# Earlier loads, copies moved to the scalar engine and re-spaced weight pieces in a DFT and mixture-of-experts kernel

## The chip, the cores and the metric

The kernel runs on one core of one Trainium2 chip, as one program. The metric is the device time of that core in microseconds (us). Its engines run beside each other, each through its own list of instructions in order, and meet at semaphores: TensorE (PE for matrix products, PEld for the loads of its stationary operand), VectorE (DVE), ScalarE (ACT), GpSimd (POOL), and SyncE (SP), which here issues nearly all DMA transfers. An instruction that waits holds up everything behind it on its engine, and a transfer that waits holds up every later transfer of SP.

## The reference

The batch is 8 sequences of 3072 tokens with 256 features, in float32.

1. A real DFT along each sequence. The spectrum is mixed by a complex 256x256 matrix (`w_r`, `w_i`) and a bias, every real and imaginary part is shrunk towards zero by 0.01, and an inverse DFT gives `y`.
2. `h = y @ w_in` (256 to 2048), `g = h - tanh(h)`, `x = g @ w_out` (2048 to 256). `w_in` and `w_out` come as float64.
3. A soft mixture of experts: logits `x @ phi` (32 slots), a softmax over all tokens to form slot inputs, eight small experts on them, and a softmax over slots to give each token its output.

## The kernel before, in words

**Phases.** `kernel_body` (L1435) runs a spectral phase (step 1), a token phase (step 2 and the logits and sums of step 3) and an expert phase. The change is all in `spectral_phase` (L125 to L631). The two are generators: the spectral one yields once per step, and beside its last steps `kernel_body` draws the first pieces of the token phase (`TOKENS_BESIDE`, L43).

**The DFT in pieces.** 3072 = 96 x 32. `f1_half` (L234) makes the 96-point part of half a piece of the input `x`; its result goes to DRAM as `ad` (a store through `flush`, L151, at the head of the next step). `load_a2` (L263) brings it back regrouped, 512 KB for two steps, into a pool of three buffers (`fa2`, L138). `f2_pair` (L275) makes the 32-point part for one step (8 small products, L281) into the PSUM bank `f2`, of which there is one. `mix_part` (L324) multiplies by the mixing matrix in three parts of six products, `add_bias` (L342) and `shrink` (L359) finish the spectrum, `i1_pair` (L374) does the first part of the inverse; its result goes to DRAM as `vd`, comes back by `load_v2` (L386) and `i2_half` (L397) does the second part into `yt`, stored as `yd`.

**The order is written by hand.** One loop, L576 to L631, has T = 96 steps (8 sequences of 12) and 12 more to drain. Step s does `f2_pair` for s, mixing, bias and shrinking for s-1, `i1_pair` for s-2, and pieces of `f1` for the next sequence and of `i2` for the one before. Each call puts its instructions at the ends of the engines' lists and its transfers at the end of SP's, so the order of calls in a step is the order on every engine. Within a step: `flush`, `f2_pair`, one chore, new chores (`narrow`), `load_x`, `mix_part` 0, `add_bias`, `load_v2`, half of `f1`, some `i2`, `fold_w`, `use_w`, `load_wf`, `split_sum`, three chores, `mix_part` 1 and 2, the other half of `f1`, `shrink`, two chores, the rest of `i2`, `i1_pair`, `store_y`, `load_a2`, `load_w`.

**The weights' pieces.** 32 pieces (16 of `w_out`, then 16 of `w_in`, L420) are prepared beside the DFT. For a piece due at step t, `load_w` (L428, at t) brings 256 KB of float64 into `raw`, of which there is one buffer; `narrow` (L497, from t+1) turns it into float32 by 11 operations of VectorE, the chores, which `pump` (L492) hands out over the steps; `use_w` (L437, at t+4) transposes it on TensorE into the bank `f2` (L453) and copies it out to `wt` (L455); `fold_w` (L466, at t+5) multiplies `wt` into the bank `f2` again and takes that out (L488 for `w_out`; L478 and L480 for `w_in`). `load_wf` (L458, at t+3) brings what the `w_in` pieces are multiplied with. The bank `f2` is thus shared by `f2_pair`, `use_w` and `fold_w`: each waits until what the one before left there has been read out.

**When things come.** A sequence's pieces of `w` are due at its steps 1, 3, 5 and 7 (L572). `load_a2` is called two steps before its data is used (L623). Before the loop, L526 to L539 make `f1` for the first sequence and load tables (`f2`, `i1`, `bias`) and the first `a2`.

Of the kernel before, what the change touches and what calls it, by code (L numbers as in the profile page):

```python
# [12 lines left out]
AF = mybir.ActivationFunctionType  # L13
ALU = mybir.AluOpType
# [110 lines left out]
def spectral_phase(tc, nb, x, w_r, w_i, b_r, b_i, tb, yd, w_in, w_out, phi, ident, wo32, md, wh, wl, wp, wy, ew):  # L125

    nc = tc.nc
    with ExitStack() as late, ExitStack() as mid, ExitStack() as ctx:
# [53 lines left out]
        def load_f2(g0, g1):  # L182
            nc.sync.dma_start(out=f2[:, 128 * g0:128 * g1], in_=tb["f2"][:, 128 * g0:128 * g1])
# [33 lines left out]
        def load_tables():  # L217
            nc.sync.dma_start(out=i1, in_=tb["i1"])
            nc.sync.dma_start(out=bias[:, 0:256], in_=b_r.partition_broadcast(128))
            nc.sync.dma_start(out=bias[:, 256:512], in_=b_i.partition_broadcast(128))  # L220
            nc.gpsimd.memset(dh.bitcast(F32), 0.0)
            nc.gpsimd.memset(dl_.bitcast(F32), 0.0)
# [214 lines left out]
        def use_w(j):  # L437
            src, r, q = pieces[j]
            t = wnew.pop(j)
            if src is w_in:  # L440
                n = slice(256 * (q % 2), 256 * (q % 2) + 256)
                if wl[r][q // 2] is None:
                    wl[r][q // 2] = ew.wp.tile([128, 512], F32R, tag=f"wl{r}{q // 2}", name="wl")
                h = wh[r][q // 2][:, n]
                nc.scalar.activation(h, t, AF.Copy)
                nc.gpsimd.tensor_tensor(
                    out=wl[r][q // 2][:, n], in0=t, in1=h.bitcast(F32), op=ALU.subtract
                )
            else:
                nc.sync.dma_start(out=wo32[128 * r:128 * r + 128], in_=t)  # L450
            pt = ps.tile([128, 2, 128], F32, tag="f2", name="pt", bufs=1)
            for k in range(2):
                nc.tensor.transpose(pt[:, k, :], t[:, 128 * k:128 * k + 128], ident)  # L453
            wt = dcp.tile([128, 2, 128], F32, tag="wt", name="wt")
            nc.vector.tensor_copy(wt, pt)  # L455
            wtr[j] = wt

        def load_wf(j):  # L458
            src, r, q = pieces[j]
            if src is w_in:  # L460

                home, tag = (ew.wp, "wl13") if j < 26 else (ew.gp, "g4")
                wf = wfs[j] = home.tile([128, 2, 256], F32, tag=tag, name="wf")
                nc.sync.dma_start(out=wf, in_=wo32[256 * q:256 * q + 256].rearrange("(k p) m -> p k m", p=128))

        def fold_w(j):  # L466

            src, r, q = pieces[j]
            wt = wtr.pop(j)
            if src is w_in:  # L470
                pw = ps.tile([128, 288], F32, tag="f2", name="pw", bufs=1)
                wf = wfs.pop(j)
                for k in range(2):
                    F = 2 * q + k
                    nc.tensor.matmul(pw[:, 0:256], wt[:, k, :], wf[:, k], start=k == 0, stop=k == 1, skip_group_check=True)
                    nc.tensor.matmul(pw[:, 256:288], wt[:, k, :], wp[:, F, :], start=False, stop=k == 1, skip_group_check=True)
                if q == 0:
                    nc.vector.tensor_scalar(out=mw, in0=pw, scalar1=-1.0, scalar2=None, op0=ALU.mult)  # L478
                else:
                    nc.vector.tensor_tensor(out=mw, in0=mw, in1=pw, op=ALU.subtract)  # L480
                if q == 7:
                    nc.sync.dma_start(out=md[128 * r:128 * r + 128], in_=mw[:, 0:256])
                    nc.vector.tensor_copy(wy[:, r], mw[:, 256:288])
                return
            pw = ps.tile([128, 32], F32, tag="f2", name="pw", bufs=1)
            for k in range(2):
                nc.tensor.matmul(pw, wt[:, k, :], ph[:, k, :], start=k == 0, stop=k == 1)
            nc.vector.tensor_scalar(out=wp[:, r, :], in0=pw, scalar1=-1.0, scalar2=None, op0=ALU.mult)  # L488

        chores = []  # L490

# [34 lines left out]
        if True:  # L526
            load_f2(0, 2)
            for i in range(8):
                for j in range(2):
                    f1_half(0, i, j)  # L530
                if i == 2:
                    load_mix()
            split_mix()
            load_a2(0, 0)
            load_f2(2, 8)
            load_tables()
            load_f2(8, 16)
            load_f2(16, NG)
            load_late_tables()  # L539
            T = nb * NP  # L540

            pieces_at = {}
            for k in range(1, nb):
                for j in range(8):
                    pieces_at[NP * (k - 1) + j + (2 if k == 1 else 0)] = (k, j)

            def piece(t):
                return [pieces_at[t]] if t in pieces_at else []

            for t in range(3):  # L550
                for j in piece(t):
                    load_x(*j)

            i2_at, v2_at, y_steps = {}, {}, {}
            for k in range(nb):
                t = NP * k + NP
                if k < nb - 2:
                    steps = [t + 4 + j for j in range(4)] + [t + 8 + j // 2 for j in range(8)] + [t + 12 + j for j in range(4)]
                    gap = 1
                else:  # L560
                    steps = [t + 4 + j // 2 for j in range(16)]
                    gap = 1
                for j in range(8):
                    for u in range(2):
                        i2_at.setdefault(steps[2 * j + u], []).append((k, j, u))
                    v2_at.setdefault(max(t + 3, steps[2 * j] - 3), []).append((k, j))
                for h in range(2):
                    for u in range(3):
                        t1 = steps[8 * h + 7] + 1 + gap * u
                        y_steps.setdefault(t1 if k < nb - 1 else T + NP - 1, []).append((k, h, 2 * u))  # L570

            slots = [NP * k + j for k in range(nb) for j in range(1, 9, 2)]  # L572
            due_w = {}
            for j in range(len(pieces)):
                due_w.setdefault(slots[len(slots) * j // len(pieces)], []).append(j)
            for s in range(T + NP):  # L576
                b, i = divmod(s, NP)
                flush()
                if s < T:
                    f2_pair(b, i)  # L580
                pump(1)
                for j in due_w.get(s - 1, ()):
                    narrow(j)
                for j in piece(s + 3):
                    load_x(*j)
                m = divmod(s - 1, NP) if 1 <= s <= T else None
                if m:
                    mix_part(*m, 0)
                    add_bias(*m)
                for j in v2_at.get(s, ()):  # L590
                    load_v2(*j)
                for j in piece(s):
                    f1_half(*j, 0)
                due = i2_at.get(s, ())
                for j in due[:(len(due) + 1) // 2]:
                    i2_half(*j)
                for j in due_w.get(s - 5, ()):
                    fold_w(j)
                for j in due_w.get(s - 4, ()):
                    use_w(j)  # L600
                for j in due_w.get(s - 3, ()):
                    load_wf(j)
                if s < T:
                    split_sum(b, i)
                pump(3)
                if m:
                    mix_part(*m, 1)
                if m:
                    mix_part(*m, 2)
                for j in piece(s):  # L610
                    f1_half(*j, 1)
                if m:
                    shrink(*m)
                pump(2)
                for j in due[(len(due) + 1) // 2:]:
                    i2_half(*j)
                if 2 <= s <= T + 1:
                    i1_pair(*divmod(s - 2, NP))
                for j in y_steps.get(s, ()):
                    store_y(*j)  # L620
                if 4 <= s < 12:
                    load_i2(s - 4)
                if s + 2 < T:  # L623
                    load_a2(*divmod(s + 2, NP))
                for j in due_w.get(s, ()):
                    load_w(j)
                if s == T:
                    ctx.close()
                if s == T + 3:
                    mid.close()  # L630
                yield  # L631
# [865 lines left out]
```

## Time and profile before

| | |
|---|---|
| three runs, us | 2300.38, 2306.78, 2307.19; median 2306.78 |
| the profiled execution's own time | 2304.85 us |
| its span, first to last instruction | 2302.7 us (2.15 us lie around it) |
| granted TensorE clock, mean over the span | 0.989 |
| busy: PE, PEld, DVE, ACT, POOL | 97%, 79%, 76%, 63%, 29% |
| the spectral steps 0 to 95 | from 28.7 to about 692 us |

How to read it: one execution was recorded. "Idle before" an instruction is the time its engine stood still ahead of it, and the arrow names whose event ended that; where several were awaited it is the one that came last. The granted clock is the share of full speed that TensorE was given: 1.0 is 2.4 GHz, 0.5 is 1.2 GHz.

### The profile page before, as it was taken

The page shows a single profiled execution, that of the slowest core. Times are in us where ns is not written, and L with a number is a line of the kernel's source. Part 1 is how long each engine was busy: PE and PEld are TensorE (multiplying, and loading weights), DVE is VectorE, ACT ScalarE, POOL GpSimd, SP SyncE. Part 2 cuts the span into 40 slices and gives each one's busy share as a digit, 9 for nine tenths or more (in the row PEclk, how much of TensorE's full clock was granted, in tenths as well). Part 3 has the DMA queues.
Part 4 walks back from the last instruction along what each step waited for, and adds up shares of the span by engine and source line. Part 5 has one row for each costly group of instructions (what it writes and reads, how often), then busy time and mean ns, then how long its engine had stood idle before and what let it go on. Part 6 is the DMA issues. An engine that isn't in the chain of part 4 may idle for free.

```text
span 2302.7 us, 51129 instructions
## 1 busy us (share of the span) xinstructions
PE 2224.2 (97%) x19832; PEld 1823.4 (79%) x19832; DVE 1761.4 (76%) x3605; ACT 1449.5 (63%) x2347; POOL 656.4 (29%) x666
## 2 busy tenths in 40 slices
PE   6899999999989999999999999999999999999989
PEld 4677777878878888888888888888887888888757
DVE  4888787888885877778777877777877787777634
ACT  2455565556545777667667676767767677666624
POOL 1333333434432422222222222222222222222111
PEclk8999999999999999999999999999999999999999
DMA  8678888888666777777777777777777777777899
GB/s 231 215 210 255 245 248 240 248 251 250 206 212 193 169 179 186 177 171 174 168 176 178 176 180 184 182 175 175 172 169 175 175 180 179 186 174 175 238 342 366
DMA packets 404018, 471.16 MB, mean 205 GB/s; under 512 B 36160, under 2 KB 351808, under 8 KB 403392
## 3 DMA queue, kind: packets, MB, share of 16 engines
q1 hardware_dynamic: 403664, 467.85, 76.7%
q8 instruction: 157, 2.57, 0.5%
q14 instruction: 85, 0.70, 0.1%
q10 hardware_dynamic: 112, 0.04, 0.0%
HBM read 164.45 MB, written 106.17 MB: 118 GB/s over the span
## 4 chain that ended last, share of the span: by engine, by line
PE 56%; DMA 6%; SPq 3%; ACT 1%; issue 0%; DVE 0%; ACTq 0%
PE ph L771 35%; PE pd L1020 7%; PE pl L892 6%; DMA yr<-yd 4%; PE p_out L1319 3%; SPq L860 3%; PE pd L812 2%; DMA ewt<-in_moe_w 2%; PE pl L828 1%; PE pl L900 1%; ACT g L782 0%; DMA gq<-in_moe_w 0%; SPq L1006 0%; DVE gt L846 0%; SPq L1308 0%
## 5 line engine op out<-in xcount | busy, mean ns | idle before, releaser
L782 ACT ACTIVATE g<-ph 128x512 f32<-128x512 f32 x752 | 448.4, 596 | 378.2 <-PE ph L771 353.4
L789 DVE TENSOR_TENSOR g<-ph,g 128x512 f32<-128x512 f32 x564 | 373.3, 676 | 157.1 <-PE ph L771 146.8
L846 DVE STREAM_TRANSPOSE gt<-g 128x512 f32<-128x512 f32 x752 | 476.1, 681 | 12.9 <-DMA gq<-gt 7.8
L771 PE MATMUL ph<-th,s 128*128 128x256 f32 x2256 | 482.0, 286 | 2.1 <-ACT g L782 2.1
L771 PEld LDWEIGHTS ph<-th,s 128*128 128x128 f32 x2256 | 377.8, 189 | 41.4 <-issue 19.4
L793 ACT ACTIVATE g<-g 128x1024 f32<-128x1024 f32 x376 | 392.6, 1054 | 1.5
L771 PE MATMUL ph<-tl,s 128*128 128x256 f32 x1128 | 318.3, 282 | 0.0
L771 PE MATMUL ph<-y,wh 128*128 128x256 f32 x1128 | 316.4, 280 | 0.0
L771 PE MATMUL ph<-yh,wl 128*128 128x256 f32 x1128 | 315.7, 280 | 0.0
L771 PE MATMUL ph<-yh,wh 128*128 128x256 f32 x1128 | 315.6, 280 | 0.0
L684 POOL TENSOR_TENSOR tl<-tr,th 128x512 fp32r<-128x512 f32 x94 | 122.1, 1300 | 383.1 <-ACT th L683 349.6
L678 POOL TENSOR_TENSOR tr<-y 128x256 f32<-128x256 f32 x92 | 68.1, 740 | 553.8 <-DMA y<-yd 553.8
L372 POOL TENSOR_TENSOR sw<-t,c 64x256 f32<-64x256 f32 x192 | 169.5, 883 | 182.2 <-DVE c L364 155.2
L771 PEld LDWEIGHTS ph<-tl,s 128*128 128x128 f32 x1128 | 213.8, 190 | 0.0
L771 PEld LDWEIGHTS ph<-yh,wh 128*128 128x128 f32 x1128 | 212.9, 189 | 0.1
L771 PEld LDWEIGHTS ph<-yh,wl 128*128 128x128 f32 x1128 | 212.4, 188 | 0.0
L771 PEld LDWEIGHTS ph<-y,wh 128*128 128x128 f32 x1128 | 212.2, 188 | 0.1
L892 PE MATMUL pl<-g,wp 128*32 128x256 f32 x3072 | 196.8, 386 | 0.0
L1020 PE MATMUL pd<-gq,et 128*32 128x512 f32 x1504 | 181.6, 593 | 0.5 <-DMA gq<-gt 0.5
L281 PEld LDWEIGHTS pf<-f,a 128*128 128x128 f32 x768 | 102.1, 198 | 94.3 <-issue 34.0
L407 PEld LDWEIGHTS pi<-i,v 96*128 96x128 f32 x1024 | 130.2, 195 | 26.1 <-issue 19.9
L281 PE MATMUL pf<-f,a 128*128 128x128 f32 x768 | 108.0, 286 | 42.8 <-DMA a<-ad 22.0
(225 smaller groups left out, 4586.3 us busy)
## 6 DMA issues: line engine op xcount, KB each, us to landing
gq<-gt SPq DMA_DIRECT2D x1504, 128.0 KB, 3.1
xt<-in_x SPq DMA_DIRECT2D x64, 384.0 KB, 5.8
vd<-vs SPq DMA_DIRECT2D x96, 256.0 KB, 4.1
v<-vd SPq DMA_DIRECT2D x64, 384.0 KB, 6.5
yd<-yt SPq DMA_DIRECT2D x48, 512.0 KB, 5.9
y<-yd SPq DMA_DIRECT2D x48, 512.0 KB, 5.9
yr<-yd SPq DMA_DIRECT2D x48, 512.0 KB, 4.1
a<-ad SPq DMA_DIRECT2D x47, 512.0 KB, 6.5
```

What stands on the lines that cost most here:

```text
L281: nc.tensor.matmul(p[:, :, h, gg, :], t[:, gg, 128 * h:128 * h + 128], f2[:, 128 * g:128 * g + 128], start=True, stop=True,)
L372: eng.tensor_tensor(out=v[64 * ri:64 * ri + 64, gg], in0=t[q, e], in1=c[q, e], op=ALU.subtract)
L407: nc.tensor.matmul(p[:, a, :], t[:, 4 * u + a, :], i2[:, 96 * n2:96 * n2 + 128], start=True, stop=True)
L684: nc.gpsimd.tensor_tensor(out=lo, in0=t, in1=hi.bitcast(F32), op=ALU.subtract)
L771: nc.tensor.matmul(o[:, 256 * j:256 * j + 256], a[u][:, 128 * j:128 * j + 128], y[v], start=new and j == 0 and k == 0, stop=n in (2, 3, 4) ...
L782: nc.scalar.activation(e[n], o.rearrange("p (j n) -> p j n", j=2), AF.Copy)
L789: nc.vector.tensor_tensor(out=h, in0=o, in1=h, op=ALU.add)
L793: nc.scalar.activation(g, g, AF.Tanh)
L846: nc.vector.transpose(out=t[:, :, 2 * (p % 4) + u, :], in_=g[:, u, :].rearrange("p (c i) -> p c i", i=32))
L860: nc.sync.dma_start(out=o[32 * q:32 * q + 32], in_=t[32 * a:32 * a + 32, q])
L892: nc.tensor.matmul(lp[c][q:q + 32, 0:256], wp[:, 2 * p + f, :], half_of(gs[c, p + f // 2][:, f % 2], h), start=p == 0 and f < 2, stop=Fals ...
L1020: nc.tensor.matmul(o[32 * a:32 * a + 32, f], ex[c][:, k, :], g[a][:, k], start=k == 0, stop=k == 3)
```

## The change

`load_a2` is called four steps ahead instead of two, save for step 12 (two); one call moves ahead of the loop, before the tables. `wt` and `wp` are copied out by ScalarE. Pieces are due at steps 0, 2, 4, 7, 10, and on every third step to 91. From step 8 on, the second `pump` of a step hands out one chore instead of two. The last `wf` tiles live in the buffer `g3` instead of `g4`.

```diff
             wt = dcp.tile([128, 2, 128], F32, tag="wt", name="wt")
-            nc.vector.tensor_copy(wt, pt)
+            nc.scalar.activation(wt, pt, AF.Copy)
...
-                home, tag = (ew.wp, "wl13") if j < 26 else (ew.gp, "g4")
+                home, tag = (ew.wp, "wl13") if j < 26 else (ew.gp, "g3")
...
-            nc.vector.tensor_scalar(out=wp[:, r, :], in0=pw, scalar1=-1.0, scalar2=None, op0=ALU.mult)
+            nc.scalar.activation(wp[:, r, :], pw, AF.Copy, scale=-1.0)
...
             load_a2(0, 0)
             load_f2(2, 8)
+            load_a2(0, 2)
             load_tables()
...
-            slots = [NP * k + j for k in range(nb) for j in range(1, 9, 2)]
-            due_w = {}
-            for j in range(len(pieces)):
-                due_w.setdefault(slots[len(slots) * j // len(pieces)], []).append(j)
+            due_w = {max(3 * j - 2, 2 * j): [j] for j in range(len(pieces))}
...
-                pump(2)
+                pump(2 if s < 8 else 1)
...
-                if s + 2 < T:
-                    load_a2(*divmod(s + 2, NP))
+
+                for t in (s + 2, s + 4):
+                    if 4 <= t < T and (t == NP) == (t == s + 2):
+                        load_a2(*divmod(t, NP))
```

## Rows read from the trace of the kernel before

**Rows 1.** The head of the profile's page: the span.

```profile
span 2302.7 us, 51129 instructions
```

**Rows 2.** Busy time by stage: from:to, width, PE, PEld, DVE, ACT, POOL, clock, DMA share, GB/s.

```profile
52.00:112.40 60.40, 53.43 (x302) 38.52 (x300) 54.59 (x119) 27.72 (x51) 22.19 (x27) 0.97 0.69 214
112.40:191.80 79.40, 76.28 (x497) 60.67 (x498) 69.93 (x146) 44.71 (x75) 30.24 (x37) 1.00 0.77 224
191.80:277.00 85.20, 81.95 (x529) 67.46 (x528) 69.71 (x146) 48.96 (x81) 30.38 (x37) 0.96 0.82 241
277.00:361.10 84.10, 80.26 (x530) 66.02 (x529) 68.97 (x146) 49.08 (x81) 30.36 (x36) 0.98 0.83 245
361.10:445.00 83.90, 81.51 (x542) 66.59 (x541) 71.06 (x145) 49.72 (x85) 33.76 (x40) 1.00 0.85 252
445.00:529.40 84.40, 82.59 (x546) 67.24 (x546) 71.84 (x146) 49.96 (x85) 33.79 (x41) 1.00 0.84 250
529.40:615.10 85.70, 82.27 (x545) 67.30 (x545) 72.19 (x147) 49.82 (x85) 33.43 (x41) 1.00 0.79 239
615.10:690.90 75.80, 69.47 (x499) 62.48 (x499) 67.11 (x131) 39.38 (x66) 30.12 (x37) 0.95 0.64 198
```

**Rows 3.** Waits of PE, 28 to 700 us: us in total, times, longest.

```profile
PE pf L281 <- DMA a<-ad: 22.0, 10, 6.9
PE pf L281 <- DVE wt L455: 9.0, 8, 1.6
PE pf L281 <- DVE t L363: 3.7, 1, 3.7
PE pf L281 <- DVE c L364: 3.5, 1, 3.5
```

**Rows 4.** Timeline, 336 to 356 us: start, duration, instruction, idle before.

```profile
338.20 1.02 SPq L269 DMA_DIRECT2D a<-ad  x1
...
340.32 0.38 PE L453 MATMUL pt<-ident,dl 128*128 128x128 f32 x2
...
344.82 0.41 DVE L455 COPY wt<-pt 128x256 f32<-128x256 f32 x1
...
347.40 1.17 PE L281 MATMUL pf<-f,a 128*128 128x128 f32 x8 [3.52 <-DVE c L364]
```

**Rows 5.** Tile a, 338.1 to 338.5 us: its one load's time to landing.

```profile
DMA to landing us min/median/max: 9.1/9.1/9.1
```

**Rows 6.** SP's own waits, 52 to 691 us: us in total, times, longest.

```profile
SPq L431 <- DVE dl L508: 150.1, 24, 8.2
```

**Rows 7.** DVE's groups by form, 52 to 691 us: busy, mean ns, idle before.

```profile
L455 DVE COPY wt<-pt 128x256 f32<-128x256 f32 x31 | 12.8, 412 | 0.0
...
L505 DVE TENSOR_SCALAR da<-raw 128x256 int32<-128x256 int32 x31 | 9.2, 297 | 29.7 <-DMA raw<-in_moe_w_out 14.9 <-DMA raw<-in_moe_w_in 14.8
...
L488 DVE TENSOR_SCALAR wp<-pw 128x32 f32<-128x32 f32 x16 | 3.0, 185 | 0.7 <-PE pw L487 0.6
```

**Rows 8.** ACT's groups by form, 52 to 691 us, the same columns.

```profile
L311 ACT ACTIVATE xmh<-xmf 128x256 fp32r<-128x256 f32 x92 | 39.0, 423 | 83.2 <-DVE xmf L304 75.0 <-DVE xmf L306 8.1
```

**Rows 9.** Timeline of the opening steps, 24 to 52 us.

```profile
34.75 0.35 SPq L431 DMA_DIRECT2D raw<-in_moe_w_out  x1
...
38.18 0.69 DVE L363 TENSOR_TENSOR t<-t,pmix 128x512 f32<-128x512 f32 x1 [1.55 <-PE pmix L322]
...
39.37 1.28 DVE L372 TENSOR_TENSOR sw<-t,c 64x256 f32<-64x256 f32 x2
...
44.81 2.05 PE L281 MATMUL pf<-f,a 128*128 128x128 f32 x8 [6.66 <-DMA a<-ad]
...
51.10 1.02 PE L379 MATMUL pi<-sw,i 128*128 128x512 f32 x2
```

**Rows 10.** Tile raw, 34.7 to 35 us: its one load's time to landing.

```profile
DMA to landing us min/median/max: 12.7/12.7/12.7
```

**Rows 11.** Tile asb, 112 to 691 us: time to landing of the 48 `ad` stores.

```profile
DMA to landing us min/median/max: 3.1/4.1/8.5
```

## The prediction

> **What bounds the kernel now.** I read the busy times by stage first. After step 95, near 692 us, the change adds and removes nothing, so whatever the spectral steps gain moves the rest of the span [rows 1] forward as it is, and only those steps have to be costed. Cut at steps 3, 12, 24 and so on, they fall into eight stretches [rows 2]. In each, what TensorE can give back is what it does not do at full speed: its idle time (width less PE busy) and the part of the width lost to the clock (width times one less the granted clock, the lower level being 1.2 instead of 2.4 GHz). In order, us: 7.0 + 1.8; 3.1; 3.3 + 3.4; 3.8 + 1.7; 2.4; 1.8; 3.4; 6.3 + 3.8. That is 31.1 idle and 10.7 of clock, 41.8 in all: the most this change can gain here without making TensorE's own work less. VectorE is next: 69 to 72 us of 79 to 86 in the middle stretches, but 54.6 of 60.4 in the first and 67.1 of 75.8 in the last.
>
> Then the waits of PE, to see what those 31 us are. Nearly all are one instruction, the first product of `f2_pair` (L281), and it has two kinds of late partner: the load of `a2` (22.0 us, of which 6.9 and 6.66 lie ahead of step 3), and VectorE, which has not yet emptied the shared bank `f2` (the copy `wt`, 9.0 us) [rows 3]. The two large waits named after `t` and `c` are loads in disguise, and the timeline of one shows it: `a2` is issued at 338.20 and lands 9.1 us later, at 347.3; PE starts at 347.40 [rows 4, 5]. `wt` was late too: its transposes ran at 340.32, and VectorE came to the copy at 344.82, over 4 us after, behind chores and shrinking.
>
> Last, SP's waits, to see why a load called two steps ahead comes late. SP stood 150.1 us, 24 times, at the load of `raw`, until the 11 chores of the piece before were done with its only buffer [rows 6]. Pieces two steps apart with chores that fill both steps mean that SP stands through most of the second one, with stores and `a2` behind it.
>
> **The change, part by part.**
>
> *`a2` four steps ahead.* A step is about 7 us (84.10 for 12, [rows 2]), so a load gains 14 us against landings of 9.1 in a bad case [rows 5]. I take all its waits from step 12 on as gone. The pool's three buffers hold two steps each; the one filled was last read a step before, so no wait is added. What is late next in those steps is `wt`, at 345.23 in the example, and that moves too. On SP each load stays behind the same transfers of its step. New is that the first load of sequences 2 to 7 now follows directly on the last `ad` store and has to wait for its landing, 4.1 us in the median [rows 11]; behind it stand only `load_w` and the next `flush`, which waits for the end of the step anyway, so I cost this at nothing; the cover is some 5.8 us, a step less about 1.2 for the store's own start.
>
> *Copies to ScalarE.* VectorE loses 32 x 0.412 + 16 x 0.185 = 16.1 us [rows 7]. ScalarE gains them at about 0.423 for 256 columns, the nearest row [rows 8]: 13.5 us, and the 16 small ones between nothing and 0.423, so 13.5 to 20.3 in all. It is busy about 50 of 84 us [rows 2] and stood 83.2 us at the very next instruction of its list (L311) waiting for VectorE [rows 8], so the copy runs in time that was idle. The waits of `f2_pair` on `wt` and `wp` then end with the transposes, several products ahead of need: gone.
> The Trainium skill, ScalarE: Activation LUTs, section Rules for kernel authors, speaks against this: simple arithmetic belongs on VectorE, up to about three times faster per element (said of bf16). This trace does not agree for float32 (423 ns against 412, [rows 7, 8]); by the page a copy would hold ScalarE some 1.24 us, an estimate, and the sum would still be as by the row, as long as L311 stands waiting.
>
> *Every third step.* The 11 chores now go out as 4, 5 and 2, and the next `raw` load is called after the last two, so SP's 150.1 us and VectorE's 29.7 at the first chore [rows 6, 7] should mostly go. VectorE's total is otherwise the same: 68.97 less 4 x 0.412 and 4 x 0.185, or 66.6 us, in the stretch from 277, against 80.26 of PE work there at most. So in the middle TensorE is left as the bound.
>
> *`g3` for `g4`.* No instruction more or less; nothing.
>
> *The opening.* The early `a2` takes away the 6.66 at step 2 [rows 9]. But piece 0 is now due at step 0: its chores enter at step 1, and three of them stand ahead of `shrink` for step 0 on VectorE. They need `raw`. In this stretch DMA runs back to back: `raw`, issued at 34.75, landed 12.7 later, at 47.45 [rows 9, 10]. In the new order it has one `a2` more (512 KB) and one `x` less (384 KB) ahead of it; at about 240 GB/s [rows 2] that is 0.6 us later, 48.0. VectorE, which did `shrink` from 38.18 to 40.65, will stand until 48.0, do three chores (about 0.4 each), then `shrink` (2.47): `sw` at 51.7. `i1_pair` started at 51.10 [rows 9]. So step 3 begins 0.6 us later, not 6.7 earlier, with VectorE some 3.5 us behind. From there to step 12 VectorE is as full as TensorE (54.6 against 53.4): less 2.4 of copies, plus the 3.5 and some four chores more, it needs the old 60 us. I take nothing for this stretch out of 8.8; bounds are -4 (the lag never caught up) and +13 (all of it, and the first 4 to 5 of step 2).
>
> *The last stretch.* Without `f1`, PE needs 69.5 less 3.8 of clock, 66 us; VectorE 67.1 less 1.2. Level, so they will wait for each other: half of 10.1, bounds 0 and 10.1.
>
> **The sum.** Opening to step 12: 0. Then 3.1, less 1 because the first steps of that stretch had no chores before and now do: 2. Then nine tenths or a little more of what is there, since small waits stay: 6.3, 5.2, 2.2, 1.6, 3.1. Last: 5. Together 25.4 us. The profiled execution took 2304.85 us (span and 2.15 around it), 1.93 under the median and 4.47 over the fastest run. 2304.85 - 25.4 = 2279.5; I say 2280.
>
> **The rivals.**
> - *The opening gains too.* If `raw` lands well before 48, or VectorE catches up, all 41.8 and about 4 of step 2 come: with a tenth kept back, 2263. For it: VectorE has idle time even there. Against: DMA is full in that stretch.
> - *VectorE takes the place.* With `f2_pair` free, PE waits for the bias, the shrinking or `mix` operands. Half the gain: 2292. Against: 66.6 of 80 in the middle [rows 2]; for it: the order within a step is tight, and the last stretch is level.
> - *SP held by `ad` (slower).* Should the landing of the last `ad` store take longer than the 5.8 us of cover, SP falls behind once per sequence, six times, and `x`, `vd` and `v` transfers come late. If 4.1 us shows on PE each time and with it a drop of the clock of 1.7 (the cost of the one in the stretch from 277): 6 x 5.8 = 35 against 25 gained, 2315. It decides where landings pass 5.8; the longest was 8.5 [rows 11], but the median is far under.
> - *It does not do what it says.* If some other wait in SP's list keeps `a2` as late as now, the copies alone leave about 2301. Against: each step's `flush` is a gate of its own, two steps are two gates.
> - *ScalarE late.* If the copy, and the wait of L311 behind it, came onto the path with two instructions' time per piece (2 x 0.423, 32 times), 27 us of the gain go and the time is 2307. Against: L311 stands waiting for longer than that in all [rows 8]. By the Trainium skill's page above (three times 0.412 less 0.412, 32 times) it would be 26 us, about the same; the trace does not bear it out.
>
> **How the numbers follow.** Forecast 0.66; opening gains 0.15; VectorE takes the place 0.11; no effect 0.03; ScalarE late 0.02; SP held 0.03. A measurement of this kernel can tell 0.3%, 6.9 us, from no change. Faster: 0.66 + 0.15 + 0.11 = 0.92; within it 0.05; slower 0.03. The range takes in the first three: the low end a little under the first rival, 2260; the high end just past the second, 2293.
>
> **What would show it.** Right: no wait of `f2_pair` on `a<-ad` or `wt` after step 12; SP's wait at `raw` cut by more than half; the clock at 1.00 from 112 to 615; the stretches of 84 us down to 78 to 82; step 96 some 25 us earlier; VectorE standing at the first chore until about 48 us. Wrong: step 12 more than 5 us before 112, or stretches unchanged with waits on `pa`, `sw` or `t` in place of `f2_pair`'s.

## The result and the profile after

The changed kernel took 2280.51 us in the median of four runs (2273.48 to 2292.09), the kernel before 2306.99 (four runs, 2300.38 to 2315.80). The ratio is 0.9885, 95% interval 0.9845 to 0.9925. The profiled execution took 2282.44 us; its span is the first line of its page:

```profile
span 2280.7 us, 51218 instructions
```

The busy times by stage, cut at the same steps as before (3, 12, 24 and so on to 95; columns as in [rows 2]):

```profile
55.20:113.80 58.60, 54.30 (x301) 39.67 (x300) 54.17 (x105) 28.50 (x58) 22.50 (x27) 0.98 0.72 218
113.80:191.50 77.70, 75.87 (x498) 61.19 (x497) 73.07 (x146) 46.44 (x85) 30.51 (x37) 1.00 0.80 231
191.50:269.60 78.10, 78.10 (x530) 64.54 (x529) 69.62 (x138) 50.17 (x89) 30.16 (x37) 1.00 0.88 262
269.60:347.90 78.30, 78.30 (x530) 64.54 (x529) 69.66 (x138) 50.29 (x89) 30.17 (x37) 1.00 0.87 264
347.90:428.60 80.70, 80.70 (x542) 66.83 (x541) 71.47 (x141) 51.24 (x90) 33.38 (x41) 1.00 0.89 263
428.60:510.10 81.50, 81.50 (x545) 67.55 (x544) 71.45 (x142) 50.93 (x89) 33.30 (x41) 1.00 0.89 258
510.10:591.70 81.60, 81.60 (x546) 67.60 (x545) 71.80 (x143) 51.00 (x89) 33.42 (x41) 1.00 0.83 252
591.70:661.20 69.50, 67.62 (x500) 60.19 (x499) 67.23 (x125) 39.11 (x69) 30.85 (x36) 1.00 0.66 208
```

From 191 to 592 us TensorE has no idle time left and the clock is never lowered. Against [rows 2] the stretches are shorter by 1.8, 1.7, 7.1, 5.8, 3.2, 2.9, 4.1 and 6.3 us; step 3 began 3.3 us later (55.26 against 51.96).

PE's waits, 28 to 668 us, the three largest:

```profile
PE pf L281 <- DMA a<-ad: 7.4, 1, 7.4
PE pi L379 <- POOL sw L372: 5.7, 5, 3.2
PE pf L248 <- DMA xt<-in_x: 4.6, 1, 4.6
```

Of the waits of [rows 3], `f2_pair` (L281) on `a2` is left once, at step 0, and on `wt` not at all. Both others are of the opening, save 0.9 us of the 5.7. How early the spectral steps end is best read from one row of the view of line L281, the start of its last product; it serves as the measure in all that follows. Before, then after:

```profile
L281 PEld LDWEIGHTS pf<-f,a x768: 186/192/333, 28.7 to 691.6; 128*128 128x128 f32 x192
```

```profile
L281 PEld LDWEIGHTS pf<-f,a x768: 186/192/338, 29.1 to 661.9; 128*128 128x128 f32 x192
```

So 29.7 us were gained up to there, and the span shrank by 22.0: from that product to the end the kernel before took 1611.1 us (2302.7 less 691.6), the changed one 1618.8. I call this the rest; it has to be explained too.

The opening, as forecast in kind: VectorE stood 11.4 us at the first chore, until `raw` landed (issued at 36.58, 13.3 us to landing), with the shrinking of step 0 behind it, and TensorE waited for that. The timelines of DVE, 36 to 60 us, and of PE, 36 to 56 us (its last row is cut off by the end of that stretch):

```profile
49.90 0.29 DVE L505 TENSOR_SCALAR da<-raw 128x256 int32<-128x256 int32 x1 [11.39 <-DMA raw<-in_moe_w_out]
...
51.95 1.28 DVE L372 TENSOR_TENSOR sw<-t,c 64x256 f32<-64x256 f32 x2
```

```profile
38.04 1.05 PE L281 MATMUL pf<-f,a 128*128 128x128 f32 x8
...
44.39 2.02 PE L248 MATMUL pf<-xt,c 96*96 96x512 f32 x2 [4.60 <-DMA xt<-in_x]
...
53.87 1.60 PE L379 MATMUL pi<-sw,i 128*128 128x512 f32 x2 [3.19 <-POOL sw L372]
55.26 1.06 PE L281 MATMUL pf<-f,a 128*128 128x128 f32 x4
```

### The profile page after: what moved, and what is told of

Same layout as the page of the kernel before. It is cut to its first block, busy times and chain, and to the rows that moved or that the text cites. A ratio compares the mean times of both kernels' runs of the same rounds, so it can differ in the third digit from the quotient of the medians.

```text
span 2280.7 us, 51218 instructions
## 1 busy us (share of the span) xinstructions
PE 2216.4 (97%) x19832; PEld 1817.4 (80%) x19832; DVE 1764.7 (77%) x3557; ACT 1456.8 (64%) x2395; POOL 656.4 (29%) x666
## 4 chain that ended last, share of the span: by engine, by line
PE 79%; DMA 9%; DVE 6%; SPq 3%; issue 2%; ACT 1%; POOL 0%; DVEq 0%; POOLq 0%; ACTq 0%
PE ph L771 35%; PE pd L1020 7%; PE pl L892 6%; PE pmix L322 5%; DMA yr<-yd 5%; PE pi L407 4%; PE pf L248 4%; PE pf L281 3%; PE p_out L1319 3%; PE pi L379 3%; SPq L860 2%; PE pa L322 2%; PE pd L812 2%; DMA ewt<-in_moe_w 1%; PE pl L828 1%
## 5 line engine op out<-in xcount | busy, mean ns | idle before, releaser
L771 PE MATMUL ph<-th,s 128*128 128x256 f32 x2256 | 482.1, 286 | 2.1 <-ACT g L782 2.1
L771 PEld LDWEIGHTS ph<-th,s 128*128 128x128 f32 x2256 | 377.8, 189 | 41.5 <-issue 19.4
L771 PE MATMUL ph<-tl,s 128*128 128x256 f32 x1128 | 318.4, 282 | 0.0
L771 PE MATMUL ph<-y,wh 128*128 128x256 f32 x1128 | 316.3, 280 | 0.0
L771 PE MATMUL ph<-yh,wl 128*128 128x256 f32 x1128 | 315.6, 280 | 0.0
L771 PE MATMUL ph<-yh,wh 128*128 128x256 f32 x1128 | 315.5, 280 | 0.0
L771 PEld LDWEIGHTS ph<-tl,s 128*128 128x128 f32 x1128 | 213.8, 190 | 0.0
L771 PEld LDWEIGHTS ph<-yh,wh 128*128 128x128 f32 x1128 | 212.9, 189 | 0.1
L771 PEld LDWEIGHTS ph<-yh,wl 128*128 128x128 f32 x1128 | 212.4, 188 | 0.0
L771 PEld LDWEIGHTS ph<-y,wh 128*128 128x128 f32 x1128 | 212.2, 188 | 0.1
L281 PEld LDWEIGHTS pf<-f,a 128*128 128x128 f32 x768 | 102.5, 195 | 54.7 <-issue 41.7
L669 POOL TENSOR_TENSOR y<-y,yh 128x1024 fp32r<-128x1024 f32 x46 | 110.5, 2402 | 121.2 <-issue 121.2
```

Of the source, the lines that this page charges most:

```text
L281: nc.tensor.matmul(p[:, :, h, gg, :], t[:, gg, 128 * h:128 * h + 128], f2[:, 128 * g:128 * g + 128], start=True, stop=True,)
L771: nc.tensor.matmul(o[:, 256 * j:256 * j + 256], a[u][:, 128 * j:128 * j + 128], y[v], start=new and j == 0 and k == 0, stop=n in (2, 3, 4) ...
```

## The experiments

The prediction gave each part of the change its own share of the waits. Theory A says the same: each part takes away its own late partner of `f2_pair`, so the shares add up. Its rival, theory B, came from the profile after: there `a2` lands 14 to 21 us before it is used in the middle steps, and two steps are only 13 us, so two steps of lead would have done as well. Then the bursts of chores were behind both late partners: VectorE fell behind in them, and SP stood at the load of `raw` until they were done. Each part was undone alone in the changed kernel, and made alone in the kernel before. Most of these runs were timed once and serve for their profiles.

**Lead undone.**

```diff
-                for t in (s + 2, s + 4):
-                    if 4 <= t < T and (t == NP) == (t == s + 2):
-                        load_a2(*divmod(t, NP))
+                if s + 2 < T:
+                    load_a2(*divmod(s + 2, NP))
...
-            load_a2(0, 2)
```

> The changed kernel with a2 called two steps ahead again (and not early in the opening). Measured by the start of the last product of f2_pair (L281): 691.6 us before, 661.9 after. Theory A, each part takes away its own late partner: a2 is late again in some 13 steps, 18 us and two or three drops of the clock come back: 680 to 687. Theory B, the bursts of chores were the cause of both late partners, since SP stood behind them: with pieces three steps apart a load called two steps ahead still lands 1 to 5 us before need (in the changed kernel it lands 14 to 18 us ahead, two steps are 13): 661 to 667, and few waits of L281 on a.

```profile
L281 PEld LDWEIGHTS pf<-f,a x768: 186/192/337, 28.8 to 660.5; 128*128 128x128 f32 x192
```

PE's waits, 28 to 700 us, have one row on `a2`:

```profile
PE pf L281 <- DMA a<-ad: 15.8, 2, 8.5
```

Two waits, both in the opening (steps 0 and 2); from 56 us on there is none. By the landings in the trace `a2` now comes 1.2 to 6.3 us before its first product from step 12 on, 13.7 to 20.7 with the lead. The lead is worth nothing once the pieces come every third step; 660.5 is even a little earlier than 661.9, and half a microsecond under theory B's range. Theory B.

**Copies undone** (`wt` and `wp` copied out by VectorE again).

```diff
-            nc.scalar.activation(wt, pt, AF.Copy)
+            nc.vector.tensor_copy(wt, pt)
...
-            nc.scalar.activation(wp[:, r, :], pw, AF.Copy, scale=-1.0)
+            nc.vector.tensor_scalar(out=wp[:, r, :], in0=pw, scalar1=-1.0, scalar2=None, op0=ALU.mult)
```

> The changed kernel with wt and wp copied out by VectorE again. Theory A: the waits of f2_pair on wt and wp come back, 10 us: 670 to 674 for the last L281 (661.9 after). Theory B: with no burst VectorE reaches the copy within its step, in the middle sequences nothing comes back, only steps up to 16 and the last eight where VectorE is as full as TensorE: 662 to 666.

The same two views:

```profile
L281 PEld LDWEIGHTS pf<-f,a x768: 186/192/338, 28.2 to 661.2; 128*128 128x128 f32 x192
```

```profile
PE pf L281 <- DVE wt L455: 5.3, 5, 1.6
```

Five waits on `wt` come back, but the end does not move. Theory B again, and a little under its range.

**Spacing undone.**

```diff
-            due_w = {max(3 * j - 2, 2 * j): [j] for j in range(len(pieces))}
+            slots = [NP * k + j for k in range(nb) for j in range(1, 9, 2)]
+            due_w = {}
+            for j in range(len(pieces)):
+                due_w.setdefault(slots[len(slots) * j // len(pieces)], []).append(j)
...
-                pump(2 if s < 8 else 1)
+                pump(2)
```

> The changed kernel with pieces due at steps 1, 3, 5 and 7 of a sequence again and two chores in the second pump. Theory A: both late partners stay cured, so nearly nothing comes back and the opening loses its wait on raw: 655 to 665 for the last L281. Theory B: VectorE has 7.3 us of work in steps of 6.5 while chores run, so TensorE now waits for the shrinking (i1_pair on sw), the bias or mix operands in those steps, 2 to 4 us per sequence: 672 to 685, with SP's wait at raw back near 150 us.

The last product, then rows of PE's waits:

```profile
L281 PEld LDWEIGHTS pf<-f,a x768: 186/192/338, 29.2 to 675.7; 128*128 128x128 f32 x192
```

```profile
PE pa L322 <- DVE t L352: 9.6, 17, 1.0
PE pf L281 <- DMA a<-ad: 7.0, 1, 7.0
PE pi L379 <- POOL sw L372: 4.2, 6, 1.4
PE pf L281 <- DVE mw L480: 3.4, 8, 0.5
```

13.8 us come back, with both late partners of `f2_pair` still cured. But this edit also puts the first piece back to step 1, and the opening gains by that. The start of step 12 before, after the change, and here:

```profile
112.36 1.16 PE L281 MATMUL pf<-f,a 128*128 128x128 f32 x8 [1.17 <-DVE wt L455]
```

```profile
113.84 1.05 PE L281 MATMUL pf<-f,a 128*128 128x128 f32 x8
```

```profile
107.67 1.05 PE L281 MATMUL pf<-f,a 128*128 128x128 f32 x8
```

From step 12 to the last product that makes 579.2, 548.1 and 568.0 us: without the opening, 20 us come back. By the busy times of these stretches some 11 of them are idle time of TensorE and 9 are longer busy time for the same products. What ends the idle time is mostly VectorE behind in the bursts: in the rows above, which take in the opening, the first product of `mix_part` waits 17 times until `add_bias` has emptied its bank `pa`. SP's wait at `raw` is 152.4 us again, as before [rows 6]. Theory B, within its range.

**Each part alone** in the kernel before. The edits are those above, turned round; the spacing takes `g3` for `g4` with it.

> The kernel before with the pieces' steps, the second pump and g3 alone changed; loads two steps ahead and copies on VectorE as before. If the bursts were the cause (theory B, as the three runs that undid one part point to), it alone brings nearly the whole gain: last L281 at 658 to 666 (691.6 before, 661.9 with the whole change). If lead and copies matter beside it (theory A), 672 or later.

```profile
L281 PEld LDWEIGHTS pf<-f,a x768: 186/192/338, 29.2 to 663.4; 128*128 128x128 f32 x192
```

> The kernel before with a2 called four steps ahead alone. Theory A: all waits on a2 go, 18 us, two or three drops of the clock (5 to 8 us) and some of the opening: 660 to 668. Theory B: in the steps in which a2 was late, wt was late too, by 0.2 to 2.2 us less, and takes the place; VectorE stays behind in the bursts: 668 to 680.

```profile
L281 PEld LDWEIGHTS pf<-f,a x768: 186/192/337, 28.1 to 679.5; 128*128 128x128 f32 x192
```

```profile
PE pf L281 <- DVE wt L455: 19.7, 17, 2.0
```

> The kernel before with the copies of wt and wp on ScalarE alone. Both theories: the waits on wt go (some 12 us with the opening's), those on a2 stay: 677 to 684. Lower than 675 would mean that 16 us less of VectorE work also lets SP come earlier.

```profile
L281 PEld LDWEIGHTS pf<-f,a x768: 186/192/338, 29.5 to 689.0; 128*128 128x128 f32 x192
```

```profile
PE pf L281 <- DMA a<-ad: 32.3, 11, 7.4
```

| part | alone: gained, us (691.6 less it) | the same from step 12 on (579.2 less it) | undone: lost, us (it less 661.9) | the same from step 12 on (it less 548.1) |
|---|---|---|---|---|
| spacing of the pieces | 28.2 | 30.2 | 13.8 | 19.9 |
| lead of `a2` | 12.1 | 7.9 | -1.4 | 1.0 |
| copies on ScalarE | 2.6 | 3.3 | -0.7 | 1.3 |

The spacing alone brings 28.2 of 29.7 us, and from step 12 on 30.2 of 31.1. The other two are poor cures for the bursts. From step 12 on they gain 7.9 and 3.3 us alone and 11.2 together (the run with the spacing undone), a little over a third of what the spacing gains alone. With the lead alone the waits on `a2` are gone but for step 0, but those on `wt` rise from 9.0 [rows 3] to 19.7 us, since the two had been late in the same steps: the missing late partner hands the step to the next. With the copies alone the waits on `wt` are gone and those on `a2` are 32.3 us against 22.0, but a second profile of the kernel before has 29.3 there, so that a hand-over in this direction is not shown. Copies alone came out worse than both theories had it, 677 to 684. Timed once each on one chip, the three gave 2283.37 (spacing), 2298.92 (lead) and 2304.98 us (copies), the kernel before 2309.36 beside them: the same order.

Every number here is one profile. The same kernel profiled twice differs by 0.7 to 1.7 us in the start of the last product, and the kernel before by 5.0 (691.6 and 696.6); counted from step 12 on, by less than 1 us and by 3.1. So shares of 1 or 2 us say nothing. The spacing itself is two edits, the steps and the one chore in the second `pump`; no run parts them, nor what SP's standing does from what VectorE's lag does.

**The opening: first pieces later.**

```diff
-            due_w = {max(3 * j - 2, 2 * j): [j] for j in range(len(pieces))}
+            due_w = {max(3 * j - 2, 2 * j + 1): [j] for j in range(len(pieces))}
```

> The changed kernel with the first pieces due at steps 1, 3, 5, 7, 10 instead of 0, 2, 4, 7, 10. In the changed kernel VectorE stands 11.4 us at the first chore, ahead of the shrinking of step 0. Theory 1, this wait is what the opening lost: i1_pair of step 0 runs some 7 us earlier, and step 12, at 113.8 after, comes at 106 to 110; last L281 at 654 to 658. Theory 2, the opening is bound by VectorE's total work whatever the order: step 12 at 112 to 115, last L281 at 660 to 663.

The last product, then the timeline of PE, 36 to 56 us:

```profile
L281 PEld LDWEIGHTS pf<-f,a x768: 186/192/337, 29.0 to 657.1; 128*128 128x128 f32 x192
```

```profile
44.52 1.02 PE L379 MATMUL pi<-sw,i 128*128 128x512 f32 x2
...
52.30 2.08 PE L379 MATMUL pi<-sw,i 128*128 128x512 f32 x2 [2.01 <-POOL sw L372]
54.17 1.79 PE L281 MATMUL pf<-f,a 128*128 128x128 f32 x8
```

`i1_pair` of step 0 runs at 44.52 instead of 53.87, step 4 begins at 54.17 (62.1 after the change), step 12 at 108.4 instead of 113.8. Theory 1: the wait at `raw`, placed ahead of the shrinking, was what the opening lost. The wait itself stays, shorter (5.0 us of VectorE against 11.4) and one step later, which the row at 52.30 shows. From step 12 on this kernel takes 548.7 us, as the changed one does. Its one time, 2285.16 us, is no better for it: the part behind the last product was the longest of all runs, 1626.3 us (see the rest of the span below).

**Later still**, with the last third of the table `f2` out of the first `x` pieces' way:

```diff
-            due_w = {max(3 * j - 2, 2 * j): [j] for j in range(len(pieces))}
+            due_w = {max(3 * j - 2, 2 * j + 2): [j] for j in range(len(pieces))}
...
-                pump(2 if s < 8 else 1)
+                pump(2 if s < 11 else 1)
...
-            load_f2(16, NG)
...
+                if s == 1:
+                    load_f2(16, NG)
```

> The changed kernel with the first pieces due at steps 2, 4, 6, 8, 10, two chores in the second pump up to step 10, and the last third of the table f2 (used from step 8) loaded in step 1 instead of ahead of the first x pieces. With the first pieces one step later still and 512 KB less ahead of the first x, the opening should have neither the wait of VectorE at raw ahead of a shrinking (8.9 us in the first chores of the run with steps 1, 3, 5) nor that of f1 on x: step 4 at 50 to 53 (54.2 there, 62.1 after the change), last L281 at 650 to 655. If VectorE's total work binds the first steps, step 12 stays at 108 and the last L281 at 656 to 658.

```profile
L281 PEld LDWEIGHTS pf<-f,a x768: 186/192/337, 28.7 to 655.8; 128*128 128x128 f32 x192
```

Step 4 began at 50.2, as expected, but step 12 at 106.6 and the last product at 655.8, between the two expectations. Some of what the opening gains is lost again by step 12: there VectorE's work counts too, as the next run shows.

**Few pieces in the first steps.** Against the run before: pieces at 2, 8, 14, then every two or three steps from 18.

```diff
-            due_w = {max(3 * j - 2, 2 * j + 2): [j] for j in range(len(pieces))}
+            due_w = {(2 + 6 * j if j < 3 else 18 + 5 * (j - 3) // 2): [j] for j in range(len(pieces))}
...
-                pump(2 if s < 11 else 1)
+                pump(2)
...
-                home, tag = (ew.wp, "wl13") if j < 26 else (ew.gp, "g3")
+                home, tag = (ew.wp, "wl13") if j < 27 else (ew.gp, "g3")
```

> The changed kernel with three pieces in the first steps (2, 8, 14) and the other 29 from step 18 every two or three steps to 88, two chores in every second pump, the last third of the table f2 loaded in step 1, wf of pieces 27 and later in g3. If the first 17 steps are bound by VectorE's work (steps of 5.6 us for TensorE, 4.2 us of VectorE without and 5.9 with a piece every third step), taking pieces out of them brings step 24 to 177 to 181 (191.5 after the change, 185.2 with the start at step 2), and the middle, where VectorE has 8 to 10 us to spare per sequence, takes them for at most 1 us each: last L281 at 645 to 651. If bursts of two steps already bring the waits of the kernel before back, 655 or later. Against the kernel before, 1.5 to 2% faster in time if the rest of the span stays.

The last product, then four stretches by stage (steps 24 to 36, and so on to 72):

```profile
L281 PEld LDWEIGHTS pf<-f,a x768: 186/192/338, 29.3 to 669.4; 128*128 128x128 f32 x192
```

```profile
177.70:261.10 83.40, 81.10 (x535) 66.30 (x534) 72.67 (x152) 50.06 (x91) 30.42 (x36) 0.98 0.84 253
261.10:340.40 79.30, 79.25 (x531) 64.95 (x530) 72.06 (x139) 49.38 (x89) 30.12 (x36) 1.00 0.83 254
340.40:429.10 88.70, 83.42 (x543) 68.43 (x542) 75.31 (x156) 50.80 (x93) 32.38 (x40) 0.98 0.84 252
429.10:512.30 83.20, 83.20 (x553) 68.93 (x552) 75.29 (x153) 50.53 (x88) 33.08 (x40) 1.00 0.80 243
```

The first half of the expectation held, step 24 at 177.7; the second failed. From step 12 on this kernel takes 569.3 us, against 549.2 of the run before. But not every stretch suffers: after the change these four took 78.1, 78.3, 80.7 and 81.5 us, and the second and fourth, though they too have pieces two and three steps apart, are 1.0 and 1.7 longer with no wait of TensorE. The other two are 5.3 and 8.0 longer. The largest wait in them is one for a load of `v`; SP's timeline and PE's, 355 to 378 us:

```profile
366.64 0.35 SPq L431 DMA_DIRECT2D raw<-in_moe_w_in  x1
...
369.12 1.41 SPq L390 DMA_DIRECT2D v<-vd  x2
```

```profile
376.22 1.73 PE L407 MATMUL pi<-i,v 96*128 96x128 f32 x8 [3.65 <-DMA v<-vd]
```

SP stood 6.7 us at this `raw`, until the last chore of the piece before was done at 366.6, and the stores and `v` stood behind it. So two pieces two steps apart can be enough of a burst: VectorE's total leaves room, but the loads behind `raw` have to wait until the piece before is done. The run changes two things at once, the steps and the chores in the second `pump` (two again), and does not tell which of them did it. The ratio to the kernel before, 0.9888 (0.9861 to 0.9915), is no better.

**The rest of the span.** The changed kernel and the kernel before once more, and the later start, timed.

> The changed kernel once more, on the same chip. Ten profiles of kernels with the same code after step 96 took 1611.8 to 1627.0 us from there to the end, most where the spectral steps ended earliest. If that part varies from run to run with the code the same, this run's last L281 is at 661 to 663 again and the rest differs from 1619.5 by some us; if it is fixed by when it starts, the rest is 1619 to 1620 again.

> The kernel before once more. Last L281 at 690 to 693. If the rest of the span varies from run to run with the code the same, it is anywhere in 1611 to 1627 us here; if it is short because the spectral steps end late, 1611 to 1613 again.

> The run with first pieces at steps 2, 4, 6, 8, 10 and then every third, once more and timed. The spectral steps should again end 4 to 7 us earlier than with the change (last L281 at 654 to 657 against 660.2 and 661.9). If the rest, which ran from 1611.8 to 1627.0 us so far, varies without regard to where the spectral steps end, the ratio to the kernel before is 0.985 to 0.988; if it gives back what is gained, 0.989 to 0.991 as with the change.

| kernel | last product, us | span, us | rest, us | of it up to the first product of L771 | PE's waits at L900 |
|---|---|---|---|---|---|
| before; again | 691.6; 696.6 | 2302.7; 2314.8 | 1611.1; 1618.2 | 52.5; 52.3 | 9.1; 14.8 |
| changed; again | 661.9; 660.2 | 2280.7; 2282.8 | 1618.8; 1622.6 | 54.0; 55.7 | 13.6; 15.1 |
| first pieces at 2, 4, 6; timed | 655.8; 656.5 | 2279.6; 2280.7 | 1623.8; 1624.2 | 54.1; 54.1 | 16.2; 18.4 |

(The expectations count the rest from the first of the step's eight products, some 0.7 us more.) The rest of one and the same kernel differs by 7.1 us before and by 3.8 after the change; the kernel before, again, ended its spectral steps 3.6 us later than the latest that was expected. Two things account for nearly all of the differences in the table. The first is the change's own. Just behind the last product, `mix_part` waits for `add_bias` on VectorE; PE's waits in the first 90 us of the rest, before and after:

```profile
PE pa L322 <- DVE t L352: 0.7, 1, 0.7
```

```profile
PE pa L322 <- DVE t L352: 2.1, 1, 2.1
```

All eight profiles with a piece on every third step have 1.8 to 2.1 us there, the others 1.0 or less. Up to the first product of L771, in the token phase, the change costs 1.5 us in the first pair of profiles.

The second is the wait of the token phase's logits (L900) for the raw `y`; PE's waits in the rest, for before, and for before again:

```profile
PE pl L900 <- DMA yr<-yd: 9.1, 19, 1.0
```

```profile
PE pl L900 <- DMA yr<-yd: 14.8, 27, 1.8
```

Without the part up to L771 and without these waits, the six rests of the table are 1549.5 to 1553.5 us. So of the 7.7 us, 1.5 are the change's own and 4.5 are waits at L900, of which the first profile of the kernel before had the least of all fourteen. These waits vary by chance, but perhaps not by chance alone: the four profiles of the three kernels described last have 16.2 to 20.6 us, the ten others 9.1 to 15.1. An early end of the spectral steps is not what sets them apart, as one of the four (few pieces in the first steps) ended at 669.4; the cause is open.

In time nothing is left of the later start's gain. It measured 0.9891 (0.9864 to 0.9918) against the kernel before, the changed kernel again 0.9893 (0.9867 to 0.9919). The expectation had 0.985 to 0.988 for a rest that varies without regard to the spectral steps and 0.989 to 0.991 for one that gives the gain back; 0.9891 lies in the second range, but the interval covers both. So 4 to 6 us less in the spectral steps make no difference in time that these runs can tell.

## Why the prediction was right, and where it was not

- *The time.* 2280 forecast, 2280.51 measured. That the two are so near is luck: four runs spread over 18.6 us, and two errors of the sum partly cancel. Up to the last product it forecast 25.4 us and 29.7 came; for what follows it forecast nothing and the profiles show 7.7 lost, which leaves 22.0.
- *"After step 95 the change adds and removes nothing".* Not quite: behind the last product `mix_part` now waits 2.1 us for VectorE instead of 0.7. And the rest varies by 7 us between two profiles of one kernel, and a sum made against a single profile takes over that profile's rest. This is the step that should have carried a range.
- *"41.8 in all: the most this change can gain here".* Too low in places: the stretch from 361 could give 2.4 by it and gave 3.2, the next 1.8 and 2.9. PE's busy time for the same products fell from 81.51 to 80.70 us and from 82.59 to 81.50. A late start shows in the busy time too: the eight products of `f2_pair` took 1.17 us behind a wait [rows 4] and 1.05 without one (the row at 38.04 above). So a width less PE busy is not the whole of what is lost.
- *The middle.* 6.3, 5.2, 2.2, 1.6 and 3.1 forecast, 7.1, 5.8, 3.2, 2.9 and 4.1 measured: right, somewhat small, in part for the reason just given.
- *The causes.* The waits were named rightly, and the reading of SP's waits (SP stands behind the chores) had the root of them. The step that failed is the division: "a load gains 14 us" and the copies were each made the cure of their own wait. The runs show that beside the spacing neither gains anything that can be told from scatter, and that without it both together gain 11.2 us from step 12 on, where the spacing alone gains 30.2.
- *"SP's 150.1 us and VectorE's 29.7 should mostly go".* SP's wait at `raw` is 100.6 us after, in 30 places instead of 24, so 3.4 us each instead of 6.3. No wait of TensorE for `a2` follows from it. From 112 us on the `flush` behind it still has to wait in about half of the places; before, in none where SP had stood. So the sign "cut by more than half" was wrong as a sign. VectorE's wait at the first chore is 16.7 us, 11.4 of it the one in the opening.
- *The opening.* Right in kind, and step 12 moved by 1.5 us against a forecast of nothing. Step 3 came 3.3 us later instead of 0.6. Most of that is the landing of `raw`, at 49.9 instead of 48.0: it was issued 1.8 us later than before (36.58 against 34.75) and took 13.3 us instead of 12.7, so that `i1_pair` started at 53.87 and not near 51.7. The last half microsecond is TensorE's clock, which had not been counted: `i1_pair` took 1.60 us instead of 1.02, with the granted clock at 0.60 from 54 to 56 us, where it was 1.00 before. That the opening could have gained, and not only stood still, is what the later start shows: 5.4 us at step 12.
- *Copies on ScalarE.* 31 copies of 400 ns in the window against 412 on VectorE, and ScalarE's busy time in the stretch from 277 rose by 1.2 us, without a wait. The Trainium skill, ScalarE: Activation LUTs, section What ACT_TABLE_LOAD costs, gives 186 ns and 0.833 per column for an activation with immediate scale and bias, which makes an estimate of 399 ns for 256 columns. The trace agrees in the mean (400, single ones 363 to 460). For the 32 columns of `wp` the estimate is 213; the trace has 235.
- *The last stretch.* 5 forecast, 6.3 measured.
- *The rivals.* "SP held by `ad`" did not come about: SP waited 8.1 us in seven such places, and PE at none. "VectorE takes the place" is what the run with the spacing undone shows, 20 us of it from step 12 on; the spacing is what kept it out. "ScalarE late" did not come about: no product waits for `wt` or `wp`. "The opening gains too" did not either, in this kernel.

## What to carry to other kernels

Where two partners of the same instruction are late by turns, look for what makes both late before giving each its own cure: here a burst of side work on one engine, behind which the queue of transfers stood as well, and spacing it out did alone what the two cures together did not. Side work in an in-order list has to be finished between the steps that need that engine, and a mean load of 85% (72 of 84 us) did not ensure that. A first piece of such work must not stand ahead of needed work while its data is still on the way.

## What was not expected of the hardware

The same program on the same kind of core takes 2273.48 to 2292.09 us, and the part of it after the spectral steps 1611.1 to 1618.2 us in two profiles of one kernel, with no drop of the clock that would explain it: loads of `y` that take 4.1 to 4.3 us in the median land up to 1.8 us late for the product of L900 in some chunks and not in others. Against that a gain of 6 us can be seen in a profile's stretch and not in a time.
